# The gate's product written to PSUM, into the free half of the first layer's bank

## The chip, the cores and the metric

The program runs on one core of one Trainium2 chip. The metric is the device time of one execution in microseconds; lower is better. The core's engines work side by side and are tied together by semaphores: TensorE (PE in the profile, with its weight loads as PEld) multiplies matrices and writes its results to PSUM; VectorE (DVE), ScalarE (ACT) and GpSimd (POOL) work element by element; SyncE (SP) issues most DMAs. All of them but DMA and GpSimd are used here with operands in PSUM; the tiles of all others lie in SBUF.

## The reference

Two parts are computed one after the other, both in float32. The first is attention with hashing: queries and keys are given a bucket from the signs of six projections, and a query sees only keys of its own bucket.

```python
q_bits = (np.einsum('bhsd,dk->bhsk', q, proj) > 0)
mask = q_bucket[:, :, :, None] == k_bucket[:, :, None, :]
scores = np.where(mask, scale * (q @ k.T), -1e9)      # 4 batches, 8 heads, 768 positions, 64 wide
attn = softmax(scores)
x = (attn @ v)                                        # put side by side: 3072 tokens x 512
```

The second is a feed-forward layer with a gate, from 512 to 2048 and back:

```python
h = x @ w_in
relu6 = np.clip(h + 3.0, 0.0, 6.0)
g = h * relu6 / 6.0
return (g @ w_out).astype(np.float32)
```

## The kernel before

**Precision by two parts.** A matmul operand is kept as two parts: a high part, which is the value rounded to the matmul's input type, and a low part, which is the value minus the high part. A product then takes three matmuls (high by high, high by low, low by high). Each operand that is made on the chip therefore costs two instructions: a copy that rounds (mostly ScalarE), and a subtraction (VectorE or GpSimd).

**Attention.** A step of the main loop handles one tile of 128 queries by 768 keys: scores on TensorE (L376, L378), the minimum on VectorE (L385), the exponential on ScalarE (L397). Probabilities then have to be transposed. In the earlier part that is done on TensorE (L407); from the interleaved stretch on it is done by a transpose of 32x32 blocks on VectorE (L418), a DMA to memory (the tile fd) and DMAs back (the tiles px and spare). Probabilities are split into parts at L464 (copy, ScalarE) and L466 or L468 (subtraction; L466 is GpSimd's, L468 is VectorE's), and multiplied with the values (L489, L501). Keys and queries of the next head are split by GpSimd (L318) and hashed (L330 to L332, L341).

**The feed-forward layer.** It goes over chunks of 256 tokens, and for each chunk over 16 slices (`fc`) of 128 hidden units. For one slice, which is called a gate below:

1. `gemm1` (L634): twelve matmuls write h, 128 hidden units by 256 tokens, into a bank of PSUM. A bank holds 512 float32 a partition, so h fills half of one.
2. `gate`: ScalarE writes relu(h + 3) to the SBUF tile g (L655). VectorE takes the minimum with 6, multiplies by h, and writes the product over g (L656).
3. `split`: ScalarE copies g, rounded, to the high part gh (L663), and the subtraction g - gh makes the low part gl (L664). Both lie in one tile, `ga` or `gb`.
4. `gemm2`: four matmuls with gh (L673, L674) and then two with gl (L678) add to the chunk's result.

**Banks.** `bank` hands out PSUM tiles under two tags, `pt` and `pu`, of two buffers each. Without a tag it alternates between the two, so four banks take turns among h, the transposes and the sums of attention. In the first feed-forward stage (`first_ffn`, batch 0) h always has the tag `pu`, so two banks take turns. A bank comes free when the last reader of its tile is through.

**SBUF tiles.** The tile g has one buffer (`tag="g", bufs=1`): the next gate's L655 writes it when its last reader is through. The tiles of the two parts have one buffer each.

**Order of the work.** The order of instructions on TensorE, VectorE, ScalarE and GpSimd is the order in which the program issues them (`tc.manual_schedule`). SP's DMAs are put in order by the planner, which works with a simulated timeline of all instructions. There are three stages in which the gate runs:

- `first_ffn`, batch 0, three chunks side by side. The weights are converted from 64-bit words in between: VectorE L194, L196, L203 and L205, ScalarE L201 and L210, GpSimd L216. In TensorE's order, gemm1 of the next gate stands ahead of gemm2 of this one. VectorE's order within a gate puts one or two conversion instructions between L656 and L664, and the others behind L664.
- the interleaved stretch (`paced`): one gate to each step of attention. In program order a step takes the value sums, then `split` of the gate of the step before (stage "A"), the splitting of probabilities, gemm1 (stage "B"), gemm2 of the gate before and `gate` (stage "C"), the next scores, and side work such as the next chunk's input (stage "D"). The subtraction in `split` is VectorE's here.
- the tail, gates alone. The subtraction is VectorE's in the last batch, and GpSimd's where `paced` is over and the batch is not the last.

`gate` is called from `first_ffn` (L863, split at once) and from `ffn` (L975, split at once or in the next step, L996).

Of the kernel before, what the change touches and what calls it, by code (L numbers as in the profile page):

```python
# [10 lines left out]
F32 = mybir.dt.float32  # L11
# [3 lines left out]
AF = mybir.ActivationFunctionType  # L15
ALU = mybir.AluOpType
AX = mybir.AxisListType

P = 128
# [24 lines left out]
def lsh_attention_moe(  # L44
# [10 lines left out]
    nc = tc.nc  # L55
    B, H, D, S = qkT.shape
# [7 lines left out]
    TC = 256  # L64
# [5 lines left out]
    sp = ctx.enter_context(tc.tile_pool(name="sp", bufs=2))  # L70
# [9 lines left out]
    paced = False  # L80
# [12 lines left out]
    def bank(shape, name: str, tag: str | None = None):  # L93

        nonlocal turn
        if tag is None:
            tag = ("pt", "pu")[turn % 2]
            turn += 1
        return ps.tile(shape, F32, name=name, tag=tag, bufs=2)
# [14 lines left out]
    three = cp.tile([P, 1], F32, name="three")  # L114
# [474 lines left out]
    def load_x(b: int, t: int, ccs: range):  # L589
        assert all(not b * H <= a[0] < b * H + ccs.stop * P // D for a in adds)  # L590
        ts = slice(t * TC, (t + 1) * TC)
        xr = wide_tile([P, NCC, TC], F32, f"xr{b}_{t}")
        of = xs[b][: len(ccs) * P, ts].rearrange("(cc p) t -> p cc t", p=P)
        if paced:
            for cc in ccs:
                pieces.append(lambda cc=cc: dma(out=xr[:, cc], in_=of[:, cc]))
            piece()
        else:
            dma(out=xr[:, : len(ccs)], in_=of)
        return xr  # L600
# [21 lines left out]
    def split_x(x, src, engine):  # L622
        multiply()
        nc.scalar.copy(x[0], src)  # L624
        engine.tensor_sub(x[1], src, x[0].bitcast(F32))  # L625

    def gemm1(n: str, fc: int, x, tag: str | None = None):
        hp = bank([P, TC], f"h{n}_{fc}", tag)
        wi = wt[2 * fc]
        terms = [(0, 0), (0, 1), (1, 0)] if tag is None else [(0, 0), (1, 0), (0, 1)]  # L630
        for k, (xp, wp) in enumerate(terms):
            for cc in range(NCC):
                wc = slice(cc * P, (cc + 1) * P)
                nc.tensor.matmul(  # L634
                    hp[:], lhsT=wi[:, wp, wc], rhs=x[cc][xp],
                    start=(k == 0 and cc == 0), stop=(k == 2 and cc == NCC - 1),
                )
        return hp

    g_turn = 0  # L640

    def gate_tiles(n: str):

        nonlocal g_turn
        g_turn += 1
        if homes or g_turn % 2:
            x = sp.tile([P, 2, TC], F32R, name=f"gb{n}", tag="gb", bufs=1)
        else:
            x = sp.tile([P, 3, TC], F32R, name=f"ga{n}", tag="ga", bufs=1)
        return x[:, 0], x[:, 1]  # L650

    def gate(n: str, fc: int, hp, copy, engine, between=lambda: None):

        g = sp.tile([P, TC], F32, name=f"g{n}_{fc}", tag="g", bufs=1)
        nc.scalar.activation(g[:], hp[:], AF.Relu, bias=three[:], scale=1.0)  # L655
        nc.vector.scalar_tensor_tensor(  # L656
            out=g[:], in0=g[:], scalar=6.0, in1=hp[:], op0=ALU.min, op1=ALU.mult
        )
        between()

        def split():
            gh, gl = gate_tiles(f"{n}_{fc}")
            copy(gh, g[:])  # L663
            engine.tensor_sub(gl, g[:], gh.bitcast(F32))  # L664
            return gh, gl

        return split
# [36 lines left out]
    def beside():  # L704
        if side:
            side.pop(0)()
# [105 lines left out]
    def first_ffn(resume):  # L812
# [30 lines left out]
        for n, (fc, t) in enumerate(order):  # L843
# [12 lines left out]
            def between():  # L856
# [3 lines left out]
                for x in [x for x in at if at[x] == 3]:  # L860
                    cv(x)

            gg = gate(f"0_{t}", fc, hp, nc.scalar.copy, nc.vector, between)()  # L863
            for x in [x for x in at if at[x] == 2]:
                cv(x)
# [29 lines left out]
    def ffn():  # L895
        nonlocal ffn_on, stage
        chunks = [(b, t) for b in range(1, B) for t in range(NTC)]
        xr, xhl = {}, {}
        pend = None

        def there(c: int) -> bool:

            return vdone >= (chunks[c][0] + 1) * HK

        def begin(c: int):
            b, t = chunks[c]
            if not spare:
                spare.append(sp.tile([P, 2 * WC], F32, name="spare", tag="ob", bufs=1))
            xr[c] = load_x(b, t, range(NCC))
            todo = scale_x(b, t, range(NCC), xr[c])  # L910
            if b < B - 1:
                side.extend([lambda: None] * (0 if paced else 2) + todo)
                return

            side.extend([lambda: None] * (4 if t else 6) + todo[:2])
            for cc in range(NCC):
                side.append(todo[2 + cc])
                side.append(lambda cc=cc: (place(c) if cc == 0 else None, split(c, cc)))

        def place(c: int):  # L920
            b, t = chunks[c]
            n = f"{b}_{t}"
            if b == B - 1 and t % 2 == 0:
                h, l = (
                    sp.tile([P, 2 * S], F32R, name=f"{x}{n}", tag=x)[:, : NCC * TC] for x in ("kk", "qq")
                )
                h, l = (x.rearrange("p (cc t) -> p cc t", cc=NCC) for x in (h, l))
            else:
                h, l = (sp.tile([P, NCC, TC], F32R, name=f"{x}{n}", tag=x, bufs=1) for x in ("xh", "xl"))
            xhl[c] = [(h[:, cc], l[:, cc]) for cc in range(NCC)]  # L930

        def split(c: int, cc: int):
            split_x(xhl[c][cc], xr[c][:, cc], (nc.vector, nc.gpsimd)[cc % 2])

        def finish():
            nonlocal pend
            which, (fc, po, gh, gl) = pend
            gemm2(fc, po, gh, gl)
            pend = None
            if fc + 1 < NFC:  # L940
                return lambda: None
            return lambda: store(*which, po, which == chunks[-1])

        for c, (b, t) in enumerate(chunks):
            while not there(c):
                if pend is not None:
                    finish()()
                stage = "B"
                yield
            n = f"{b}_{t}"  # L950
            if c not in xr:
                begin(c)
            while side:
                beside()
                stage = "B"
                yield
                if not paced:
                    yield
            if c not in xhl:
                place(c)  # L960
                for cc in range(NCC):
                    split(c, cc)
            ffn_on = True
            copy = nc.scalar.copy
            po = None
            for fc in range(NFC):
                hp = gemm1(n, fc, xhl[c])
                stage = "C"
                yield
                end = finish() if pend is not None else lambda: None  # L970
                if po is None:
                    po = ps.tile([P, 2, 512], F32, name=f"po{n}", tag="s" if b == B - 1 and t % 2 == 0 else "po", bufs=1)
                parted = paced
                engine = nc.vector if b == B - 1 or paced else nc.gpsimd
                split_g = gate(n, fc, hp, copy, engine)  # L975
                if not parted:
                    gg = split_g()
                end()
                if c + 1 < len(chunks) and c + 1 not in xr and there(c + 1):
                    if fc >= XF[chunks[c + 1][0] == B - 1]:  # L980
                        begin(c + 1)
                if parted:
                    stage = "D"
                    yield
                    for _ in range(-(-len(side) // (NFC - fc))):
                        beside()
                if fc + 1 == NFC and c + 1 in xr and c + 1 not in xhl and not side:
                    place(c + 1)
                    for cc in range(NCC):
                        split(c + 1, cc)  # L990
                elif not parted:
                    beside()
                if parted:
                    stage = "A"
                    yield
                    gg = split_g()  # L996
                pend = ((b, t), (fc, [po[:, u] for u in range(2)], *gg))
                stage = "B"
                yield
                if not parted:  # L1000
                    beside()
            del xhl[c]
        finish()()
# [33 lines left out]
    load_w(0)  # L1037
    raws[0] = raw0
    fill = ffn()
    vnext = 0  # L1040

# [25 lines left out]
    with tc.manual_schedule(engines={ET.PE, ET.DVE, ET.Activation, ET.Pool}):  # L1067
# [155 lines left out]
        paced = False  # L1223
# [51 lines left out]
```

## Time and profile before

Three runs took 994.56, 996.15 and 998.57 us; their median is 996.15. The profiled execution took 998.63 us, of which the span from its first to its last instruction is 996.9 us; the granted clock of TensorE was 0.995 of full speed over the span.

| engine | busy us | share of the span | instructions |
|---|---|---|---|
| TensorE, matmul | 960.8 | 96% | 6330 |
| TensorE, weight load | 876.7 | 88% | 6330 |
| VectorE | 741.2 | 74% | 1437 |
| ScalarE | 632.0 | 63% | 1419 |
| GpSimd | 497.8 | 50% | 521 |

The four instructions of the gate that are not matmuls:

| line | engine | what | count | busy us | mean ns |
|---|---|---|---|---|---|
| L655 | ScalarE | relu(h + 3) to g | 192 | 90.8 | 473 |
| L656 | VectorE | min with 6, times h, to g | 192 | 80.1 | 417 |
| L663 | ScalarE | high part, to gb / ga | 139 / 53 | 56.4 / 21.6 | 406 / 407 |
| L664 | VectorE | low part, to gb / ga | 136 / 49 | 79.5 / 22.4 | 584 / 457 |
| L664 | GpSimd | low part | 7 | 5.2 | |

How rows are read: a row of a group gives line, engine, operation, output tile and input tiles, shapes and count, then the group's busy time in us and the mean of one instruction in ns, then the engine's idle time before them with what ended it. A row of the timeline gives start and length in us, and in brackets the idle time before it and its releaser. A row of waits reads "engine, line, waited for whom: us in total, times, longest". A row of a window gives start and end, length, busy us with the number of instructions for each engine, then the granted clock, the DMA engines' share and GB/s. The chain of waits follows back from the last instruction, at each step to what released it. PE's busy time is modelled: a matmul's end lies up to 0.16 us past the moment at which the next may start.

### The profile page before, as it was taken

How to read it: one execution, taken by the hardware profiler on the slowest of the kernel's cores; microseconds unless marked ns; L12 is line 12 of the kernel's file. 1: busy time of each engine (PE TensorE's matmuls, PEld its weight loads, DVE VectorE, ACT ScalarE, POOL GpSimd, SP SyncE). 2: the span in 40 equal slices, each digit the busy share in tenths (PEclk: the TensorE clock that was granted, in tenths of full speed). 3: DMA queues.
4: the chain of work that ended last, by engine and by line, in shares of the span. 5: the costliest groups of instructions: out<-in, count | busy, mean ns of one | idle time of the engine just before them, and what ended most of it. 6: DMA issues, size and time to landing. Idle time of an engine off the chain costs nothing.

```text
span 996.9 us, 19351 instructions
## 1 busy us (share of the span) xinstructions
PE 960.8 (96%) x6330; PEld 876.7 (88%) x6330; DVE 741.2 (74%) x1437; ACT 632.0 (63%) x1419; POOL 497.8 (50%) x521
## 2 busy tenths in 40 slices
PE   8999999999999999799989999999999999999997
PEld 7999889888889998689879898888989989899996
DVE  7999988988579999777877878878887863243322
ACT  6888866555478888566666676666766663333332
POOL 6777745556546776455645645645645542100100
PEclk9999999999999999999999999999999999999999
DMA  4566689000045554478787787778887670101000
GB/s 121 140 154 172 149 249 369 2 2 1 6 131 116 120 124 122 127 230 233 218 256 230 229 241 236 232 224 251 241 242 234 186 227 14 43 1 43 1 22 22
DMA packets 109980, 148.51 MB, mean 149 GB/s; under 512 B 13380, under 2 KB 79300, under 8 KB 109880
## 3 DMA queue, kind: packets, MB, share of 16 engines
q1 hardware_dynamic: 105320, 141.64, 46.8%
q0 software_dynamic: 4560, 5.64, 4.6%
q8 instruction: 50, 0.82, 0.3%
q14 instruction: 50, 0.41, 0.1%
HBM read 75.76 MB, written 52.04 MB: 128 GB/s over the span
## 4 chain that ended last, share of the span: by engine, by line
PE 62%; DVE 16%; DMA 5%; issue 5%; POOL 5%; ACT 4%; SPq 3%; DVEq 0%; ACTq 0%; POOLq 0%
PE h L634 18%; PE acc L489 6%; PE po L678 5%; PE po L673 5%; PE po L674 5%; PE pt L407 5%; PE s L376 4%; PE s L378 4%; PE acc L501 4%; DVE p L385 4%; SPq L78 3%; DVE pl L468 3%; DMA spare<-fd 2%; POOL pl L466 2%; DMA px<-fd 2%
## 5 line engine op out<-in xcount | busy, mean ns | idle before, releaser
L397 ACT ACTIVATE p<-p,m 128x768 f32<-128x768 f32 x192 | 180.2, 938 | 89.7 <-DVE p L385 79.8
L385 DVE TENSOR_SCALAR_CACHE_REDUCE p<-s 128x768 f32<-128x768 f32 x192 | 182.9, 953 | 41.9 <-PE s L378 26.7
L656 DVE SCALAR_TENSOR_TENSOR g<-g,h 128x256 f32<-128x256 f32 x192 | 80.1, 417 | 103.9 <-ACT g L655 102.4
L655 ACT ACTIVATE g<-h,three 128x256 f32<-128x256 f32 x192 | 90.8, 473 | 94.8 <-PE h L634 80.1
L634 PE MATMUL h<-xh,w 128*128 128x256 f32 x1024 | 146.3, 282 | 2.9 <-ACT xh L624 2.9
L634 PEld LDWEIGHTS h<-xh,w 128*128 128x128 f32 x1024 | 135.5, 189 | 6.5 <-ACT xh L624 3.1
L466 POOL TENSOR_TENSOR pl<-spare,ph 128x384 fp32r<-128x384 f32 x43 | 59.3, 1379 | 121.6 <-ACT ph L464 74.6
L418 DVE STREAM_TRANSPOSE p<-p 128x768 f32<-128x768 f32 x86 | 84.0, 976 | 42.9 <-ACT p L397 42.8
L663 ACT CAST gb<-g 128x256 fp32r<-128x256 f32 x139 | 56.4, 406 | 81.2 <-DVE g L656 51.7
L468 DVE TENSOR_TENSOR pl<-pt,ph 128x384 fp32r<-128x384 f32 x204 | 104.0, 549 | 3.7 <-ACT ph L464 3.2
L376 PE MATMUL s<-kk,qq 76*128 76x384 f32 x384 | 102.2, 347 | 3.3 <-DVE qq L341 1.8
L378 PE MATMUL s<-kk,qq 128*128 128x384 f32 x384 | 101.2, 345 | 0.0
L464 ACT CAST ph<-pt 128x384 fp32r<-128x384 f32 x204 | 89.8, 473 | 16.1 <-PE pt L407 12.9
L673 PE MATMUL po<-w,gb 128*128 128x512 f32 x246 | 97.1, 395 | 1.5 <-ACT gb L663 1.4
L216 POOL TENSOR_TENSOR w<-wr,w 128x128 fp32r<-128x128 f32 x128 | 73.7, 609 | 47.2 <-ACT w L210 45.4
L674 PE MATMUL po<-w,gb 128*128 128x512 f32 x246 | 96.9, 394 | 0.0
L407 PE MATMUL pt<-ident,p 128*128 128x128 f32 x636 | 89.9, 275 | 5.1 <-DVE pl L468 4.3
L664 DVE TENSOR_TENSOR gb<-g,gb 128x256 fp32r<-128x256 f32 x136 | 79.5, 584 | 18.8 <-ACT gb L663 18.3
L407 PEld LDWEIGHTS pt<-ident,p 128*128 128x128 f32 x636 | 75.3, 141 | 13.2 <-PE pt L407 4.0
L634 PE MATMUL h<-xl,w 128*128 128x256 f32 x512 | 83.7, 283 | 2.6 <-POOL xl L625 2.2
L466 POOL TENSOR_TENSOR pl<-px,ph 128x384 fp32r<-128x384 f32 x43 | 56.7, 1318 | 54.7 <-ACT ph L464 38.8
L678 PE MATMUL po<-w,gb 128*128 128x512 f32 x246 | 78.3, 399 | 3.3 <-DVE gb L664 3.1
(156 smaller groups left out, 2167.3 us busy)
## 6 DMA issues: line engine op xcount, KB each, us to landing
fd<-p SPq DMA_DIRECT2D x86, 384.0 KB
spare<-fd SPq DMA_DIRECT2D x172, 96.0 KB
px<-fd SPq DMA_DIRECT2D x172, 96.0 KB
kk<-qq SPq DMA_DIRECT2D x62, 192.0 KB
wr<-in_w_in SPq DMA_DIRECT2D x16, 512.0 KB
wr<-in_w_out SPq DMA_DIRECT2D x16, 512.0 KB
raw<-in_qkT SPq DMA_DIRECT2D x20, 384.0 KB
vr<-in_v SPq DMA_DIRECT2D x32, 192.0 KB
```

The lines of the kernel that those rows point to most:

```text
L376: nc.tensor.matmul(s[:, c, :HW], lhsT=q1[:KM, us], rhs=half(k1[:KM], c), start=True, stop=False)
L378: nc.tensor.matmul(s[:, c, :HW], lhsT=q2[:, us], rhs=half(k2, c), start=False, stop=True)
L385: nc.vector.tensor_scalar(out=pr_[:], in0=s[:, :, :HW], scalar1=CAP, scalar2=None, op0=ALU.min, op1=ALU.min, accum_out=m[:],)
L397: nc.scalar.activation(pr_[:], pr_[:], AF.Exp, bias=m[:], scale=-1.0, accum_out=sms[b][:, t, h : h + 1])
L407: nc.tensor.transpose(pt[:, x], probs[g][0][:, c, x * P : (x + 1) * P], ident[:])
L466: engine.tensor_sub(lo, pt, hi.bitcast(F32))
L468: lows.append(lambda: engine.tensor_sub(lo, pt, hi.bitcast(F32)))
L634: nc.tensor.matmul(hp[:], lhsT=wi[:, wp, wc], rhs=x[cc][xp], start=(k == 0 and cc == 0), stop=(k == 2 and cc == NCC - 1),)
L655: nc.scalar.activation(g[:], hp[:], AF.Relu, bias=three[:], scale=1.0)
L673: nc.tensor.matmul(po[u], lhsT=gh[:, us], rhs=wo[:, 0], start=(fc == 0), stop=False)
L674: nc.tensor.matmul(po[u], lhsT=gh[:, us], rhs=wo[:, 1], start=False, stop=False)
L678: nc.tensor.matmul(po[u], lhsT=gl[:, us], rhs=wo[:, 0], start=False, stop=(fc == NFC - 1))
```

## The change

The tile that `gemm1` allocates becomes a whole bank, two halves of 256; h is the first half. `gate` still lets ScalarE write the relu to an SBUF tile (now r, with the tag that g had), but VectorE's product goes to the second half of h's bank. Both parts are made from there: L663 and L664 read g in PSUM. [...] The bank is held until L664 is through; the SBUF tile only until the product is written. The number of instructions is the same.

```diff
     def gemm1(n: str, fc: int, x, tag: str | None = None):
-        hp = bank([P, TC], f"h{n}_{fc}", tag)
+        hg = bank([P, 2, TC], f"h{n}_{fc}", tag)
+        hp = hg[:, 0]
...
-                    hp[:], lhsT=wi[:, wp, wc], rhs=x[cc][xp],
+                    hp, lhsT=wi[:, wp, wc], rhs=x[cc][xp],
...
-        return hp
+        return hg
...
-    def gate(n: str, fc: int, hp, copy, engine, between=lambda: None):
-
-        g = sp.tile([P, TC], F32, name=f"g{n}_{fc}", tag="g", bufs=1)
-        nc.scalar.activation(g[:], hp[:], AF.Relu, bias=three[:], scale=1.0)
-        nc.vector.scalar_tensor_tensor(
-            out=g[:], in0=g[:], scalar=6.0, in1=hp[:], op0=ALU.min, op1=ALU.mult
-        )
+    def gate(n: str, fc: int, hg, copy, engine, between=lambda: None):
+
+        hp, g = hg[:, 0], hg[:, 1]
+        r = sp.tile([P, TC], F32, name=f"g{n}_{fc}", tag="g", bufs=1)
+        nc.scalar.activation(r[:], hp, AF.Relu, bias=three[:], scale=1.0)
+        nc.vector.scalar_tensor_tensor(out=g, in0=r[:], scalar=6.0, in1=hp, op0=ALU.min, op1=ALU.mult)
         between()
 
         def split():
             gh, gl = gate_tiles(f"{n}_{fc}")
-            copy(gh, g[:])
-            engine.tensor_sub(gl, g[:], gh.bitcast(F32))
+            copy(gh, g)
+            engine.tensor_sub(gl, g, gh.bitcast(F32))
             return gh, gl
...
-                engine = nc.vector if b == B - 1 or paced else nc.gpsimd
-                split_g = gate(n, fc, hp, copy, engine)
+                split_g = gate(n, fc, hp, copy, nc.vector)
```

## The prediction

> **What bounds the kernel now.** I read the page first: the shares of the engines, the slices, the chain that ended last.
>
> ```profile
> span 996.9 us, 19351 instructions
> PE 960.8 (96%) x6330; PEld 876.7 (88%) x6330; DVE 741.2 (74%) x1437; ACT 632.0 (63%) x1419; POOL 497.8 (50%) x521
> ...
> PE   8999999999999999799989999999999999999997
> ...
> PE 62%; DVE 16%; DMA 5%; issue 5%; POOL 5%; ACT 4%; SPq 3%; DVEq 0%; ACTq 0%; POOLq 0%
> ```
>
> TensorE is busy almost everywhere, so a faster VectorE gains only where TensorE waits for it. I therefore cut the run at the stages in which the gate runs: the first feed-forward stage (145 to 263 us), the stretch with attention and gates interleaved (424 to 845), and the tail of gates alone (845 to the end). Columns are length, then busy us (instructions) of PE, PEld, DVE, ACT, POOL. The second fence is the same for line 664 alone, the subtraction that makes the gate's low part (DVE, POOL).
>
> ```profile
> 145.00:263.00 118.00, 116.44 (x731) 103.60 (x730) 103.12 (x201) 68.91 (x144) 69.02 (x117) 1.00 0.26 94
> 424.00:845.00 421.00, 410.50 (x2632) 372.23 (x2632) 324.98 (x579) 269.20 (x620) 223.41 (x201) 1.00 0.75 220
> 845.00:997.00 152.00, 145.56 (x934) 130.40 (x932) 49.47 (x121) 53.47 (x121) 10.66 (x19) 0.99 0.06 22
> ```
> ```profile
> 145.00:263.00 118.00, 21.96 (x41) 0.00 (x0) 1.00 0.26 94
> 424.00:845.00 421.00, 55.42 (x89) 2.96 (x4) 1.00 0.75 220
> 845.00:997.00 152.00, 20.45 (x48) 2.21 (x3) 0.99 0.06 22
> ```
>
> In the tail one L664 costs 20.45/48 = 426 ns; in the interleaved stretch 55.42/89 = 623 ns, in the first stage 536 ns. Same work, longer. The durations (minimum/median/maximum) of L664 and of L656, which forms the product, and then two places in the timeline, show why:
>
> ```profile
> L664 DVE TENSOR_TENSOR gb<-g,gb x136: 411/426/1945, 145.6 to 986.7; 128x256 fp32r<-128x256 f32 x136
> L656 DVE SCALAR_TENSOR_TENSOR g<-g,h x192: 401/421/424, 144.7 to 988.7; 128x256 f32<-128x256 f32 x192
> ```
> ```profile
> 428.24 1.83 POOL L318 TENSOR_TENSOR qq<-raw,qq 64x768 fp32r<-64x768 f32 x1
> 428.41 1.95 DVE L664 TENSOR_TENSOR gb<-g,gb 128x256 fp32r<-128x256 f32 x1
> ...
> 429.35 0.39 PE L674 MATMUL po<-w,gb 128*128 128x512 f32 x1
> ...
> 430.41 0.73 PE L678 MATMUL po<-w,gb 128*128 128x512 f32 x2 [0.67 <-DVE gb L664]
> ...
> 639.40 1.42 POOL L466 TENSOR_TENSOR pl<-px,ph 128x384 fp32r<-128x384 f32 x1 [1.37 <-ACT ph L464]
> 639.99 0.42 DVE L656 SCALAR_TENSOR_TENSOR g<-g,h 128x256 f32<-128x256 f32 x1
> ```
>
> At 428.41 L664, both inputs in SBUF, starts while GpSimd subtracts, and ends only 0.29 us after GpSimd does (430.07 to 430.36); TensorE's L678 waits. At 639.99 L656, one input in SBUF and one in PSUM, runs through a GpSimd subtraction undisturbed, and in all 192 cases it never exceeds 424 ns. After the change L664 has exactly L656's kind of inputs.
>
> **The change part by part.** *L664 no longer waits for GpSimd.* At 426 ns instead of 623 and 536 it saves DVE 89 x 0.197 + 41 x 0.110 = 22 us of busy time. What of it reaches the end, by stage:
>
> In the **first stage** the chain runs through VectorE, not TensorE. Its pieces (start, length) over two repeats, the ends of the stretch in which the piece recurs, and the tail for comparison:
>
> ```profile
> 168.32 0.61 DVE gb L664
> ...
> 186.19 0.61 DVE gb L664
> ...
> 191.77 0.60 DVE gb L664
> 192.37 0.64 DVE wr L196
> ...
> 197.91 0.61 DVE gb L664
> ...
> 250.41 0.61 DVE gb L664
> ...
> 861.88 1.40 PE h L634 x12
> ...
> 870.27 0.82 PE h L634 x7
> ```
>
> 186.19 to 197.91 is one repeat of four gates, 11.72 us; the tail does three gates in 870.27 - 861.88 = 8.39, so four in 11.19. From 168.32 to 250.41 stand 82.1/11.73 = 7 repeats: TensorE can regain at most 7 x 0.54 = 3.8 us. Each repeat has two slow L664 in its chain:
>
> ```profile
> 189.98 5.14 POOL L216 TENSOR_TENSOR w<-wr,w 128x128 fp32r<-128x128 f32 x8 [3.46 <-ACT w L210]
> ...
> 191.69 0.69 DVE L664 TENSOR_TENSOR gb<-g,gb 128x256 fp32r<-128x256 f32 x1
> ...
> 192.30 0.96 DVE L196 SCALAR_TENSOR_TENSOR wr<-wr 128x512 uint32<-128x512 uint32 x1
> ```
>
> Each gives back 0.69 - 0.43 = 0.26. But at 192.30 the next instruction, L196, also reads two SBUF tensors, and GpSimd's row of L216 is still going on: it would inherit part of the wait. I count 0.26 for one of the two and 0.16 for the other (an estimate), 0.42 a repeat: **-3.0 us** (bounds -3.8 and 0).
>
> In the **interleaved stretch** TensorE's idle time names the term:
>
> ```profile
> PEld po L678 <- DVE gb L664: 7.8, 11, 1.2
> ...
> PE po L678 <- DVE gb L664: 3.1, 5, 0.8
> ...
> PE po L673 <- ACT gb L663: 1.4, 1, 1.4
> ```
>
> 3.1 us in five waits; the idle figure leaves out the modelled end of the matmul before (L674 to L678 is 1.06 us at 429.35, 0.23 at full pitch, so 0.83 lost where 0.67 stands): 5 x 0.16 more, 3.9. From above, the chain: L664 is on it here seven times while slow, first and last
>
> ```profile
> 428.49 1.88 DVE gb L664
> ...
> 807.53 0.50 DVE gb L664
> ```
>
> and the excess of these seven over 426 ns adds up to 6.1 us. What is late next are attention's DMA and GpSimd (L466, L625), which a shorter L664 doesn't hasten, so I take **-3.5 us** (bounds -6.1 and 0).
>
> *The tail*: no term. TensorE has no wait there for L664; its cover is gemm2's first four matmuls. *The seven L664 on GpSimd* (4 + 3 in the windows) go to VectorE, busy 49.47 of 152 us there: nothing.
>
> *Inputs and outputs in PSUM.* The rows that bear on it:
>
> ```profile
> L468 DVE TENSOR_TENSOR pl<-pt,ph 128x384 fp32r<-128x384 f32 x204 | 104.0, 549 | 3.7 <-ACT ph L464 3.2
> L468 DVE TENSOR_TENSOR pl<-spare,ph 128x384 fp32r<-128x384 f32 x43 | 22.4, 522 | 4.6 <-ACT ph L464 4.4
> L663 ACT CAST gb<-g 128x256 fp32r<-128x256 f32 x139 | 56.4, 406 | 81.2 <-DVE g L656 51.7 <-PE po L678 29.1
> L572 DVE TENSOR_TENSOR xr<-xr,rt 128x256 f32<-128x256 f32 x45 | 18.5, 413 | 3.6 <-PE rt L569 3.5
> L531 ACT COPY y<-acc 128x256 f32<-128x256 f32 x86 | 31.7, 369 | 9.2 <-PE acc L489 7.3
> ```
>
> A subtraction that reads PSUM is 27 ns longer at 384 wide (L468), one of 256 is 413 against L664's 426: bounds -13 and +27, I take 0. ScalarE's copy from PSUM is 369 against 406: 0.04 us less, on the chain once a repeat in the first stage and in the last gate, so 0.3 us in all, which I leave inside the bounds.
>
> [...]
>
> *L656 writes PSUM, into the bank that it reads.* No VectorE or ScalarE row here writes PSUM. Bounds: 0, and a second cycle for each element, (549 - 413)/128 = 1.06 ns, so +0.27 us; below nothing, -0.04, as ScalarE's gain on the PSUM side. I take 0: L656 is the same instruction on the same bank, and the matmuls write these banks at full pitch.
>
> *The bank is held longer*, until L664 rather than L656. Four banks take turns, in the first stage two. In TensorE's order gemm2 of a gate, which already waits for its L664, stands ahead of the matmuls that come into that bank next, so the new wait is covered; without that cover it would be the 0.85 us of a copy and a subtraction. *The SBUF tile* of the relu is now free after L656: ScalarE's wait for it in the first stage goes (11.3 us below), off the path, as L656 stands behind VectorE's conversion anyway.
>
> ```profile
> ACT g L655 <- DVE gb L664: 11.3, 15, 1.0
> ```
>
> Sum: -3.0 - 3.5 = -6.5. The profiled execution took 998.63 us (span 996.9, 1.7 around it), so 992.1; it lies 2.5 above the median of the runs, 996.15, from which the same sum gives **989.7 us**, my forecast.
>
> **The rivals.**
>
> *A gain hidden behind attention.* If the next late thing (L466's subtraction, a landing) takes over each wait of the stretch, and L196 inherits the first stage's, 0 to 3 us are left: 993 to 996. For it: DMA, POOL and SP's queue together hold 13% of the whole chain (first fence). Against: the five waits of L678 are TensorE's own, and nothing else stands behind them.
>
> [...]
>
> *Slower: L656 in one bank takes two cycles an element.* +0.27 us, four times a repeat: +1.08 against -0.42, so 7 x 0.66 = +4.6 in the first stage, and in the stretch 93 x 0.27 = 25 us of VectorE against 17 saved, with L385 queued behind it: the gain there gone and about 1 us more. 1001.8. From +0.11 us per L656 the first stage no longer gains; from about +0.28 the whole is over 0.5% slower.
>
> *SP's order changes.* SP's queue is ordered by the planner, which is given other instructions; nothing in the profile says which way that goes. A late landing costs TensorE about 1.4 us (L673 <- L663 above, behind a wait for a landing); a few more or fewer of them: 990 to 1001.
>
> **How the numbers follow.** Chances: forecast 0.56 (its own range 986.5 to 992.5), hidden 0.22, PSUM operand 0.07, two cycles 0.06, SP's order 0.09. About 0.5%, 5 us, is what can be told from no change, so the border of faster is 991.2: 0.43 of the forecast, 0.02 of hidden, 0.01 and 0.02 of the others make 0.48; slower (above 1001.1) 0.05 and 0.02 make 0.07; the rest 0.45. Range: from 986, with both upper bounds (996.15 - 3.8 - 6.1 = 986.3), to 997.5, no gain and the spread of the runs.
>
> **What would show it.** L664 at most about 430 ns in every stage, on DVE alone; L656 still about 420; no wait of L678 for L664; the first stage's four gates in about 11.2 us, not 11.7; L196's mean up a little. Wrong: L656 near 0.69 us; L664 still over 1 us under a GpSimd subtraction; a matmul of L634 that waits for L664; or all of these right and the span unmoved, with DMA or L466 longer on the chain.

## The result and the profile after

The changed kernel takes 991.49 us, the median of 7 runs from 990.71 to 993.35; the kernel before, 997.62 us over 7 runs beside it. The ratio is 0.9943 with a 95% interval of 0.9928 to 0.9957: 0.57% faster, about 5.7 us (the two medians differ by 6.1), where the prediction's sum was 6.5. The profiled execution took 993.35 us, its span is 991.6. In the kernel after, gemm1 is line 635, the relu L657, the product L658; the copy and the subtraction are still L663 and L664.

The page of the kernel after: span, engines, the chain that ended last, and the groups of the product and of the copy.

```profile
span 991.6 us, 19371 instructions
PE 957.5 (97%) x6330; PEld 877.2 (88%) x6330; DVE 716.1 (72%) x1444; ACT 626.4 (63%) x1419; POOL 491.2 (50%) x514
...
PE 71%; DVE 9%; DMA 7%; POOL 4%; issue 3%; SPq 3%; ACT 2%; DVEq 0%; ACTq 0%; POOLq 0%
...
L658 DVE SCALAR_TENSOR_TENSOR h<-g,h 128x256 f32<-128x256 f32 x192 | 82.0, 427 | 108.2 <-ACT g L657 106.6
...
L663 ACT CAST gb<-h 128x256 fp32r<-128x256 f32 x139 | 51.6, 372 | 75.6 <-DVE h L658 45.6
```

VectorE is busy 25 us less, and its share of the chain fell from 16% to 9%; TensorE's rose from 62% to 71%. The product costs 427 ns instead of 417 now that it is written to PSUM, the copy 372 instead of 406. The subtraction, by its durations (minimum/median/maximum):

```profile
L664 DVE TENSOR_TENSOR gb<-h,gb x139: 409/420/426, 145.8 to 982.0; 128x256 fp32r<-128x256 f32 x139
...
L664 DVE TENSOR_TENSOR ga<-h,ga x53: 411/425/426, 149.3 to 984.8; 128x256 fp32r<-128x256 f32 x53
```

All 192 are VectorE's now, with g in PSUM and the high part in SBUF as inputs, and take 409 to 426 ns, where up to 1945 stood before. **Where the 5.3 us of span came from** is read from the first matmul of the 1st, the 41st, the 49th and the 141st gate. Up to the 41st, batch 0's weights are converted in between; the 49th opens the interleaved stretch, and the 141st is past its end. The timeline of the kernel before, then of the kernel after:

```profile
142.54 0.40 PE L634 MATMUL h<-xh,w 128*128 128x256 f32 x2
...
257.88 0.28 PE L634 MATMUL h<-px,w 128*128 128x256 f32 x1
...
419.31 0.39 PE L634 MATMUL h<-xh,w 128*128 128x256 f32 x1 [2.87 <-ACT xh L624]
...
840.38 0.28 PE L634 MATMUL h<-xh,w 128*128 128x256 f32 x1
```
```profile
142.78 0.28 PE L635 MATMUL h<-xh,w 128*128 128x256 f32 x1
...
254.19 0.28 PE L635 MATMUL h<-px,w 128*128 128x256 f32 x1
...
415.60 0.38 PE L635 MATMUL h<-xh,w 128*128 128x256 f32 x1 [2.67 <-ACT xh L624]
...
835.47 0.40 PE L635 MATMUL h<-xh,w 128*128 128x256 f32 x2
```

The first stage went from 115.34 to 111.41 us, 3.9 less. Between it and the stretch nothing moved (161.43 and 161.41). The stretch went from 421.07 to 419.87, 1.2 less. The rest nearly cancels: 0.2 longer ahead of the first gate, 0.4 shorter behind the 141st. In the first stage the chain of the kernel after is TensorE's alone:

```profile
184.41 1.40 PE h L635 x12
...
195.60 0.47 PE h L635 x4
```

184.41 to 195.60 is four gates, 11.19 us, the tail's pace; before they took 11.72, on VectorE. In the stretch most of TensorE's idle time changed its name. Its waits (us in total, times, longest) between 415 and 840 us, before and then after:

```profile
PE po L678 <- DVE gb L664: 3.1, 5, 0.8
...
PE s L376 <- DVE qq L341: 1.8, 5, 0.4
PE po L673 <- ACT gb L663: 1.4, 1, 1.4
PE acc L501 <- POOL pl L466: 0.5, 2, 0.2
...
PE acc L501 <- ACT ph L464: 0.2, 1, 0.2
```
```profile
PE s L376 <- DVE qq L341: 2.3, 3, 1.5
...
PE acc L501 <- POOL pl L466: 1.6, 7, 0.3
PE po L678 <- DVE gb L664: 1.6, 2, 1.1
PE acc L501 <- ACT ph L464: 1.0, 1, 1.0
...
PE po L673 <- ACT gb L663: 0.2, 1, 0.2
```

L678 and L673 together lost 2.7 us of waits; L466, L464 and L341 gained 1.1 + 0.8 + 0.5 = 2.4. Two traces alone can't say what of this is the change's. Six of the experiments below give traces of the same window: three have the stretch as before (first stage alone, free tile, memset in the kernel before), three have the product in PSUM there (the rest alone, memset in the kernel after, SP's order). Over these and the two above, TensorE waited in us for

| what is waited for | stretch as before, four traces | product in PSUM, four traces |
|---|---|---|
| the subtraction L664 | 3.0 to 3.7 | 0.3 to 1.9 |
| GpSimd's L466 | 0.4 to 0.9 | 1.3 to 1.6 |
| ScalarE's L464 | at most 0.4 | 0.7 to 1.2 |

These three move clear of their spread. The waits of L673 and those for L341 overlap, and are not shown to have moved.

What L678 still waits for is no longer GpSimd's work:

```profile
508.47 0.96 DVE L385 TENSOR_SCALAR_CACHE_REDUCE p<-s 128x768 f32<-128x768 f32 x1 [1.75 <-DMA fd<-p]
...
509.35 0.42 DVE L664 TENSOR_TENSOR gb<-h,gb 128x256 fp32r<-128x256 f32 x1
...
509.83 0.50 PE L678 MATMUL po<-w,gb 128*128 128x512 f32 x1 [1.14 <-DVE gb L664]
```

L664 takes its 0.42 us, but starts late, behind L385, which waited 1.75 us for the DMA that carries a transposed tile (fd from p). That DMA comes late in part by the planner's new order on SP's queue (see the experiment on it).

### The profile page after: what moved, and what is told of

Same layout as the page of the kernel before. It is cut to its first block, busy times and chain, and to the rows that moved or that the text cites. A ratio compares the mean times of both kernels' runs of the same rounds, so it can differ in the third digit from the quotient of the medians.

```text
span 991.6 us, 19371 instructions
## 1 busy us (share of the span) xinstructions
PE 957.5 (97%) x6330; PEld 877.2 (88%) x6330; DVE 716.1 (72%) x1444; ACT 626.4 (63%) x1419; POOL 491.2 (50%) x514
## 4 chain that ended last, share of the span: by engine, by line
PE 71%; DVE 9%; DMA 7%; POOL 4%; issue 3%; SPq 3%; ACT 2%; DVEq 0%; ACTq 0%; POOLq 0%
PE h L635 23%; PE acc L489 6%; PE po L678 6%; PE po L673 6%; PE po L674 6%; PE pt L407 5%; PE s L376 4%; PE s L378 4%; PE acc L501 4%; DMA px<-fd 3%; SPq L78 3%; DVE p L385 3%; DVE pl L468 3%; POOL pl L466 2%; DMA spare<-fd 2%
## 5 line engine op out<-in xcount | busy, mean ns | idle before, releaser
L385 DVE TENSOR_SCALAR_CACHE_REDUCE p<-s 128x768 f32<-128x768 f32 x192 | 182.9, 953 | 44.3 <-PE s L378 25.7
L658 DVE SCALAR_TENSOR_TENSOR h<-g,h 128x256 f32<-128x256 f32 x192 | 82.0, 427 | 108.2 <-ACT g L657 106.6
L657 ACT ACTIVATE g<-h,three 128x256 f32<-128x256 f32 x192 | 90.8, 473 | 100.0 <-PE h L635 98.2
L466 POOL TENSOR_TENSOR pl<-spare,ph 128x384 fp32r<-128x384 f32 x43 | 59.1, 1375 | 114.1 <-ACT ph L464 80.1
L464 ACT CAST ph<-pt 128x384 fp32r<-128x384 f32 x204 | 89.5, 472 | 16.6 <-PE pt L407 13.6
L663 ACT CAST gb<-h 128x256 fp32r<-128x256 f32 x139 | 51.6, 372 | 75.6 <-DVE h L658 45.6
L673 PE MATMUL po<-w,gb 128*128 128x512 f32 x246 | 96.9, 394 | 0.2 <-ACT gb L663 0.2
L216 POOL TENSOR_TENSOR w<-wr,w 128x128 fp32r<-128x128 f32 x128 | 71.8, 591 | 45.3 <-ACT w L210 42.5
L466 POOL TENSOR_TENSOR pl<-px,ph 128x384 fp32r<-128x384 f32 x43 | 58.4, 1357 | 60.0 <-ACT ph L464 40.1
L376 PEld LDWEIGHTS s<-kk,qq 76*128 76x128 f32 x384 | 65.6, 190 | 16.4 <-DVE qq L341 6.8
L678 PE MATMUL po<-w,gb 128*128 128x512 f32 x246 | 77.4, 395 | 1.6 <-DVE gb L664 1.6
```

Source lines behind the costliest of these rows:

```text
L376: nc.tensor.matmul(s[:, c, :HW], lhsT=q1[:KM, us], rhs=half(k1[:KM], c), start=True, stop=False)
L385: nc.vector.tensor_scalar(out=pr_[:], in0=s[:, :, :HW], scalar1=CAP, scalar2=None, op0=ALU.min, op1=ALU.min, accum_out=m[:],)
L466: engine.tensor_sub(lo, pt, hi.bitcast(F32))
L657: nc.scalar.activation(r[:], hp, AF.Relu, bias=three[:], scale=1.0)
L673: nc.tensor.matmul(po[u], lhsT=gh[:, us], rhs=wo[:, 0], start=(fc == 0), stop=False)
L678: nc.tensor.matmul(po[u], lhsT=gl[:, us], rhs=wo[:, 0], start=False, stop=(fc == NFC - 1))
```

## The experiments

The theory was that GpSimd's subtraction keeps L664 waiting while L664 reads two SBUF tiles; that this set the first stage's pace; and that in the stretch other late work takes over. The rivals: the SBUF tile that is free earlier; the planner's order on SP's queue; the stretch as the place of the gain.

**One stage at a time.** `gate` gets a switch, and the product goes to PSUM in one caller only (here the first stage's; the second kernel is the mirror image):

```diff
...
-                split_g = gate(n, fc, hp, copy, nc.vector)
+                engine = nc.vector if b == B - 1 or paced else nc.gpsimd
+                split_g = gate(n, fc, hp, copy, engine, psum=False)
```

> The product goes to PSUM in the first feed-forward stage only; from the interleaved stretch on it goes to the SBUF tile as before. The stages' gains add up if the first stage's gain is its own: by the two traces the first stage gave 3.9 us and the stretch 1.2, so this kernel should be 3.9 us faster than before (ratio 0.996), with four gates of the first stage in 11.2 us instead of 11.7 and the slow subtractions of the stretch (up to about 1.9 us) still there. Rival, that the stretch is what counts (as 3.5 of my 6.5 us said): at most 3 us faster. Rival, that a change of the planner's order on SP's queue made the gain: no gain here, if that order is as before.

> The other part alone: the product goes to the SBUF tile in the first feed-forward stage, and to PSUM in the interleaved stretch and the tail. By the two traces 1.2 us faster than before (ratio 0.9988), which is close to what can't be told from nothing; by the prediction's term for the stretch 3.5 us faster (0.9965). The waits of the matmuls L678 for the subtraction should be gone in both cases, and by the first view other waits of TensorE (for GpSimd's L466, for VectorE's L341 behind a late landing) should have grown by about as much.

The first stage alone: ratio 0.9961 (0.9947 to 0.9974), 3.9 us faster. The rest alone: 0.9983 (0.9967 to 0.9999), 1.7 us. Together 5.6, about what the whole change gives (5.7). The first kernel's trace has the stage at the new length, from the 1st gate to the 41st 111.41 us:

```profile
142.00 0.28 PE L635 MATMUL h<-xh,w 128*128 128x256 f32 x1
...
253.41 0.28 PE L635 MATMUL h<-px,w 128*128 128x256 f32 x1
```

By the middle values the first stage is worth more than the rest; the two intervals overlap. In the second kernel the first stage is as long as before (115.24 us), and TensorE's waits moved as in the kernel after: L680, its line for L678, from 3.1 to 1.9, and

```profile
PE po L680 <- DVE gb L666: 1.9, 2, 1.6
...
PE acc L501 <- POOL pl L466: 1.4, 6, 0.3
PE rt L569 <- POOL spare L559: 1.2, 1, 1.2
PE acc L501 <- ACT ph L464: 0.9, 2, 0.8
```

I had expected the waits of L678 to go to nothing. They did not.

A single trace says little of the stretch: in the four traces with the subtraction as before in the stretch it takes 419.57 to 421.26 us, in the four with the product in PSUM 418.07 to 419.87.

**The tile that is free earlier.** The kernel before, with a tile of its own for the relu in the first stage:

```diff
+        r = sp.tile([P, TC], F32, name=f"r{n}_{fc}", tag="y2", bufs=1) if two else g
-        nc.scalar.activation(g[:], hp[:], AF.Relu, bias=three[:], scale=1.0)
+        nc.scalar.activation(r[:], hp[:], AF.Relu, bias=three[:], scale=1.0)
         nc.vector.scalar_tensor_tensor(
-            out=g[:], in0=g[:], scalar=6.0, in1=hp[:], op0=ALU.min, op1=ALU.mult
+            out=g[:], in0=r[:], scalar=6.0, in1=hp[:], op0=ALU.min, op1=ALU.mult
```

> The kernel before, except that in the first feed-forward stage the relu goes to an SBUF tile of its own, so that ScalarE's next relu no longer waits for the subtraction L664 (11.3 us of waits before); L664 still reads two SBUF tiles. If the gain of the first stage comes from L664 not being kept out by GpSimd: no change (ratio 1.000, within 0.15%), L664 still about 0.69 us under GpSimd's subtraction, four gates still in 11.7 us. Rival, that it comes from the tile that is free earlier: 3.9 us faster (0.996), four gates in 11.2 us.

Ratio 1.0017 (1.0002 to 1.0032): no gain, a little slower if anything. The subtraction (here line 665) is as slow as before, 21.98/41 = 536 ns, and the stage as long, 115.42 us. The view by windows, for this line alone (window, its length, VectorE's busy time and instructions, GpSimd's, granted clock, DMA's share, GB/s), and the timeline:

```profile
145.00:263.00 118.00, 21.98 (x41) 0.00 (x0) 1.00 0.27 96
```
```profile
143.36 0.28 PE L634 MATMUL h<-xh,w 128*128 128x256 f32 x1
...
258.78 0.28 PE L634 MATMUL h<-px,w 128*128 128x256 f32 x1
```

ScalarE's waits for L664 are gone from this trace. The 11.3 us that it waited for the tile were off the path, as the prediction had it, and this rival is out.

**GpSimd without its subtractions.** In the kernel before and in the kernel after, GpSimd's subtractions of the weights give way to a memset:

```diff
-        for c in range(0, WC, P):
-            c = slice(c, c + P)
-            nc.gpsimd.tensor_sub(w[:, 1, c], hf[:, c], w[:, 0, c].bitcast(F32))
+        nc.gpsimd.memset(w[:, 1].bitcast(F32), 0.0)
```

> The kernel before, with GpSimd's four subtractions L216 for each weight tile replaced by one memset of zeros: GpSimd then writes the tile and reads no SBUF for it. The low part of the weights is left out of the result. If it is GpSimd's reading of SBUF that keeps L664 out in the first stage, L664 is about 0.43 us there, four gates take 11.2 us, and the kernel is about 4 us faster than before (0.996). If L664's slowness there has another cause (ScalarE's copy, a late high part), it stays near 0.69 us and nothing is gained.

> The same memset in place of L216, in the kernel after (low part of the weights left out). If the change works in the first stage by freeing L664 from GpSimd's reads, there is nothing left for it to free: the first stage is as long as in the kernel before with the memset (within 0.3 us), and the kernel is only about 1 us faster than that one, from the stretch. If the change gains in the first stage by something else (the SBUF tile, the faster copy from PSUM), the two still differ by about 4 us there.

> The kernel before with GpSimd's memset in place of L216 (low part of the weights left out) once more, for its trace: the profiled execution before this one was disturbed throughout. As expected there: L664 about 0.43 us in the first stage, four gates in 11.2 us, if it is GpSimd's reads of SBUF that keep L664 out; 0.69 and 11.7 if not.

The kernel before with the memset: 0.9962 (0.9950 to 0.9975), about as much as the change itself gives in that stage. Its second trace shows L664 (here L662) at 17.28/42 = 411 ns in the first stage, though it still reads two SBUF tiles, and the stage at 112.05 us:

```profile
145.00:260.00 115.00, 17.28 (x42) 0.00 (x0) 1.00 0.28 98
```
```profile
142.12 0.28 PE L632 MATMUL h<-xh,w 128*128 128x256 f32 x1
...
254.17 0.28 PE L632 MATMUL h<-px,w 128*128 128x256 f32 x1
```

The kernel after with the memset: 0.9940 (0.9920 to 0.9960), no faster than the kernel after alone, with 111.99 us for the stage (143.26 to 255.25). With GpSimd's subtractions gone, the change has nothing left to give in this stage: 112.05 against 111.99. Both are 0.6 us longer than the 111.41 of the kernel after, and all of that lies in the last gate: from the 1st gate to the 40th the memset kernels take 108.68 and 108.62 us, the kernel after 108.61, the kernel before 112.54. In that last gate one L203 takes 2.76 us (2.70 in the other kernel) beside another GpSimd instruction, L274. So both ways reach the same 3.9 us.

The memset does more than stop GpSimd's reads of SBUF: one memset of 0.53 us stands where four subtractions stood, and none of the L664 of the stage lies beside one. So L664 alone can't tell whether GpSimd's reads or its mere work keep it out. L196 can, which also reads two SBUF tensors: in each of the two traces nine of them run beside nearly the whole of a memset in 678 to 687 ns, as long as those beside none (676 to 689), where one beside L216 took up to 958 in the kernel before:

```profile
189.91 0.68 DVE L196 SCALAR_TENSOR_TENSOR wr<-wr 128x512 uint32<-128x512 uint32 x1
190.06 0.53 POOL L214 MEMSET w<- 128x512 f32 x1 [1.69 <-ACT w L210]
```

In the kernel before, an L216 that starts 0.18 us into an L196 (at 156.97) leaves that L196 at 684 ns, but takes 831 ns itself, where the shortest takes 455. The memset shown, which starts 0.15 us into its L196, takes 0.53 us: neither kept the other waiting.

The memset frees the conversion of the weights too: L205 takes 685 ns there on average, and 789 in the kernel before. In the kernel after it still takes 788, so the change did not need that: its 3.9 us came with L664, and with a shorter L196 (below). ScalarE's copy is 34 ns shorter when it reads PSUM, and stood 14 times on the chain of the stage before, so at most some 0.5 us of the gain could be its own (an estimate); that was not tried alone. Two inputs in SBUF are not what marks an instruction that GpSimd can hold up: L203, with one, takes 409 to 422 ns in the kernel before when GpSimd does nothing, and 429 to 986 beside its instructions.

**Landings** (the moments at which a DMA's data have arrived). In both kernels, three of the four DMAs that bring a transposed tile back are left out, with the tiles cleared once at the start:

```diff
-            for x in range(4):
+            for x in range(1):
                 r = slice(32 * x, 32 * x + 32)
                 dma(
```

> The kernel before, with attention's way back from memory cut to a quarter in the interleaved stretch: of the four DMAs that bring a transposed tile back only the first is issued, the other three quarters of the tile stay zero. The landings come earlier and SP's queue has some 250 DMAs less. If the stretch is limited by landings beside TensorE, it gets shorter by 3 to 8 us. If TensorE and VectorE alone limit it: less than 2 us.

> The same cut (three of four DMAs back left out) in the kernel after. If the late landings took over the waits that the change removed from the stretch, the change is worth more here: this one is 6 to 8 us faster than the kernel before with the same cut, 3.9 from the first stage and 2.5 to 4 from the stretch. If the stretch had never much to gain (the waits of L678 were already covered), the difference stays near 5 us.

With the cut the kernel before is at 0.9961 (0.9945 to 0.9976), the kernel after at 0.9887 (0.9865 to 0.9909), medians 994.44 and 987.00. So the way back through memory does limit the stretch: 3.9 us in the one, 5.6 (0.9943 less 0.9887) in the other. The cut shortens SP's queue and takes away traffic as well as bringing landings forward, and these were not told apart. The change is worth 7.4 us under the cut, inside what I expected if landings took over, but the intervals of the two ratios leave 5.7 possible. The traces put the stretch at 416.06 and 414.13 us, 1.9 apart where 1.2 stood without the cut, and this 0.7 is less than the 1.7 by which traces of an unchanged stretch differ. That landings are a part of what took over is suggested by this, not shown.

**SP's order.** The order of the two programs shows that the planner did change SP's queue, in two places. This puts one DMA back:

```diff
...
+                g = {22: 126, 30: 174}.get(i)
+                if nr == 2 and g in fds:
+                    with tc.issue_after(fds[g].ins):
+                        dma(out=to.bitcast(F32), in_=q1[r].bitcast(F32))
...
```

> The kernel after, with SP's queue held closer to the order of the kernel before: the planner had put one DMA of a head's keys (kk from qq) ahead of a transposed tile's DMA (fd from p) in two places; here it comes behind it again. (One piece of the next chunk's input stays one place later in both.) If the planner's order has no part in the result: the same time as the kernel after (ratio to before 0.994, within 0.2%). If it cost the stretch the gain that I had expected there: about 2 us faster than after (0.992). If the order is what gained: about 1 to 2 us slower than after (0.996).

0.9938 (0.9918 to 0.9957) against 0.9943: the runs can't tell the two apart, and the 0.992 of an order that cost 2 us lies inside the interval. The trace speaks for a cost in the stretch, which takes 418.07 us, 1.8 less than in the kernel after. At the place shown above, where the planner had put the keys' DMA ahead of the tile's (502.06 and 502.75 us), L385 (here L390) now waits half as long, and L678 (here L685) 0.33 us instead of 1.14:

```profile
506.59 0.96 DVE L390 TENSOR_SCALAR_CACHE_REDUCE p<-s 128x768 f32<-128x768 f32 x1 [0.87 <-DMA fd<-p]
...
507.94 0.73 PE L685 MATMUL po<-w,gb 128*128 128x512 f32 x2 [0.33 <-DVE gb L671]
```

So part of what L678 still waited for was the new order; whether that costs the whole run anything stays open. The order is not what gained: the kernel with the change in the first stage alone has the old order throughout and has that stage's whole gain. What the moved piece of input would do was not tried.

**Two ways to use VectorE's free time.** First the low parts of the next chunk's input, all by VectorE in the stretch:

```diff
-            split_x(xhl[c][cc], xr[c][:, cc], (nc.vector, nc.gpsimd)[cc % 2])
+            split_x(xhl[c][cc], xr[c][:, cc], nc.vector if paced else (nc.vector, nc.gpsimd)[cc % 2])
```

> The kernel after, with the low parts of the next chunk's input (L625) made by VectorE alone in the interleaved stretch, where GpSimd made half of them. TensorE's waits for GpSimd's L625 (3.7 us lost in both kernels) should go; VectorE, 17 us freer there, gets 7 us more. If TensorE's waits there are GpSimd's alone: 2 to 3 us faster than after (0.9915). If the next late thing (landings, L466) takes over again: the same as after (0.994).

> The kernel before, with the low parts of the next chunk's input (L625) made by VectorE alone in the interleaved stretch; the gate's product stays in SBUF. If that edit's gain (2 us in the kernel after) is its own, this is 2 to 3 us faster than before (0.9975). If it needs the VectorE time that the change freed (17 us in the stretch), it gains nothing here or loses (1.000 or more), since L625's extra instructions on VectorE stand beside gate subtractions that still wait for GpSimd.

In the kernel after: 0.9915 (0.9898 to 0.9931), median 989.42, the fastest of those that leave nothing out, some 2.8 us beyond the change, and the stretch 415.90 us instead of 419.87. In the kernel before: 0.9967 (0.9954 to 0.9981), 3.3 us, so this gain doesn't need the change. But in both kernels the planner also moved some eight to ten other DMAs of SP's queue in the stretch, and what part of the gain is theirs was not told apart. Why the edit is cheap for VectorE is seen in the durations of L625 (output xl) in the stretch, in the kernel after and then in this one:

```profile
L625 DVE TENSOR_TENSOR xl<-xr,xh x10: 809/956/2052, 487.2 to 792.5; 128x256 fp32r<-128x256 f32 x10
L625 POOL TENSOR_TENSOR xl<-xr,xh x10: 726/911/919, 488.0 to 793.1; 128x256 fp32r<-128x256 f32 x10
```
```profile
L625 DVE TENSOR_TENSOR xl<-xr,xh x20: 409/410/2052, 487.8 to 789.1; 128x256 fp32r<-128x256 f32 x20
```

Side by side the two took 956 and 911 ns; GpSimd's alone takes 732 (median of four in the tail). VectorE by itself does twice as many at 410, some 0.8 us for two where a pair took about 0.95. The 2052 in both rows lies beside another GpSimd subtraction, L318.

Second, the queries' half of L318:

```diff
+                engine = nc.vector if paced and r.start == 0 else nc.gpsimd
                 for c in spans(i + 1):
-                    nc.gpsimd.tensor_sub(to[:, c], raw[r, c], q1[r, c].bitcast(F32))
+                    engine.tensor_sub(to[:, c], raw[r, c], q1[r, c].bitcast(F32))
```

> The kernel after, with half of the low parts of keys and queries (the queries' half of L318, 1.84 us each on GpSimd) made by VectorE in the interleaved stretch. GpSimd then comes earlier to L466, for which TensorE's value sums wait. If GpSimd's queue is what is late next: 1 to 3 us faster than after (0.992). Rival: VectorE's instruction has two SBUF inputs and waits for GpSimd as L664 did before, in front of L385 and L418, and the kernel is 1 to 4 us slower than after (0.996 or more).

0.9990 (0.9979 to 1.0002): the change's gain is nearly gone, the stretch takes 425.07 us, 5.2 more than in the kernel after, and the time is what the rival forecast. VectorE's instruction (here L319) takes 1.31 us, and the waits for L466 (here L467), which it was to shorten, grew to twice those of the kernel after:

```profile
L319 DVE TENSOR_TENSOR qq<-raw,qq x13: 1043/1311/1320, 423.1 to 767.2; 64x768 fp32r<-64x768 f32 x13
```
```profile
PE acc L502 <- POOL pl L467: 3.4, 14, 0.3
```

All 13 lie beside a GpSimd L467 in the trace. What part of the loss is VectorE's longer queue, what part GpSimd being kept waiting, and what part the two places in which the planner moved SP's DMAs was not told apart.

## Why the prediction was right

- **The sum** was -6.5 us; the runs give -5.7, within the range and on the side forecast. That it came so near is in part luck: the first stage's term was 0.9 us too small and the stretch's 1.8 to 2.3 too large, and the two largely cancel. The mechanism was right.
- **L664 freed from GpSimd** (at most about 430 ns in every stage): right, 409 to 426, and VectorE's busy time fell by 25 us where 22 were foreseen. Shown by three kernels: with the product in PSUM, with GpSimd's subtractions gone, and with a free SBUF tile alone, which did nothing.
- **First stage, -3.0**: under-sized, 3.9 by the kernel with that stage alone. The step that failed is the discount for L196, which was to inherit part of the wait. Its mean was to go up a little; it fell, from 812 to 755 ns over the whole run, and GpSimd's L216 became shorter too:

```profile
L216 POOL TENSOR_TENSOR w<-wr,w 128x128 fp32r<-128x128 f32 x128 | 73.7, 609 | 47.2 <-ACT w L210 45.4 <-DMA wr<-in_w_in 1.7
...
L196 DVE SCALAR_TENSOR_TENSOR wr<-wr 128x512 uint32<-128x512 uint32 x32 | 26.0, 812 | 0.0
```
```profile
L216 POOL TENSOR_TENSOR w<-wr,w 128x128 fp32r<-128x128 f32 x128 | 71.8, 591 | 45.3 <-ACT w L210 42.5 <-DVE gb L664 2.4 <-DVE wr L203 0.3
...
L196 DVE SCALAR_TENSOR_TENSOR wr<-wr 128x512 uint32<-128x512 uint32 x32 | 24.2, 755 | 0.0
```

  The upper bound, TensorE's own pace, is what decided: 11.19 us for four gates, and 3.8 for the seven repeats.
- **Stretch, -3.5**: over-sized, 1.2 in the trace and 1.7 (0.1 to 3.3) in the kernel with that part alone. The step that failed is "nothing else stands behind them": it took TensorE's waits for L664 as gone, and as gained. They went down from 3.1 us to 1.6, not to nothing, and over the eight traces the waits for L466 and L464 grew by about 0.9 and 0.7 us. The rival "a gain hidden behind attention" came nearer for this stage, and was wrong for the first. A single trace is a weak witness here: the stretch of the kernel with the first stage alone, where nothing was changed in it, measures 419.71 us against 421.07 before. The upper bound of this term, 6.1, counts the whole length of the seven slow L664; their pieces on the chain exceed 426 ns by 5.3 in all. The forecast does not hang on it.
- **Nothing for the tail, the bank and the SBUF tile**: right as far as the traces show. From the 141st gate to the end 156.5 us became 156.1; none of TensorE's waits in the stretch after is gemm1's for L664; the kernel with the free tile gained nothing.
- **The price of PSUM**: 0 taken for L656, +10 ns measured (417 to 427), far from +0.27 us; 0 for L664's PSUM operand, and 420 or 425 measured against 422 or 426 undisturbed before. No run shows a dearer L664 with an operand in PSUM, which had a chance of 0.07, nor 0.27 us more for L656, which had 0.06: both are out.
- **SP's order**: the planner changed it in two places. It lengthened one wait of L678 that the trace shows; the runs can't tell whether it cost time.

## What to carry to other kernels

Look at the spread of one instruction's duration, not at its mean. Here a VectorE instruction whose maximum was over four times its median (L664, 1945 against 426 ns), next to a sister with one PSUM input that never moved (L656, 401 to 424), was waiting for GpSimd; whether the slow ones lie beside a GpSimd instruction is seen in the timeline (here all 51 above 430 ns do). In this kernel three things freed such an instruction: one input in PSUM (L664, 409 to 426 ns), a neighbour on GpSimd that only writes (L196 beside the memset, 678 to 687 ns where up to 958 stood), and both halves of a pair on VectorE (L625, a median of 410 ns where 956 stood). Price the gain at the pace of the next engine in each stage: it was whole where TensorE stood close behind with no other wait (3.9 us in the first stage), and partly handed on where GpSimd's L466 and ScalarE's L464 came late next (1.2 us in the stretch's trace).

## What was not expected of the hardware

Two subtractions, side by side on VectorE and GpSimd, were slower as a pair (956 and 911 ns) than both on VectorE alone (410 each). And one execution of the kernel before with the memset took 2381.99 us, where its others lie between 993.42 and 995.92; it happened to be the first one profiled, and it is left out of the ratio. The page of that trace:

```profile
span 2380.2 us, 19255 instructions
PE 2371.8 (100%) x6330; PEld 1943.1 (82%) x6330; DVE 713.1 (30%) x1437; ACT 650.3 (27%) x1419; POOL 428.5 (18%) x425
...
L632 PE MATMUL h<-xh,w 128*128 128x256 f32 x1024 | 341.9, 531 | 0.0
```

A matmul of gemm1 takes 531 ns instead of 282 there and TensorE is busy throughout, while VectorE's busy time is about as in the second trace of this kernel (713.1 against 724.8 us) and the granted clock reads 1.000. The cause is not known.
